# Ten loads of the transfer queue moved later in a fused attention and feed-forward kernel

## The chip, the cores and the metric

The kernel runs on one core of one Trainium2 chip. The metric is the device time of one execution in microseconds (us); the median of several runs is compared. A profile of one execution shows where the time goes.

## The reference

The kernel computes an attention of two parts and feeds its output, token by token, into a feed-forward layer. Per batch (8) and head (8), with 576 positions and a head size of 64:

```python
q_d = q.reshape(B, H, Sd, 4, D).mean(axis=3)        # the same for k and v: pooled by four
out_d = sm_attn(q_d, k_d, v_d)                      # softmax attention of 144 x 144
out_up = np.repeat(out_d, 4, axis=2)
mask = np.abs(pos[:, None] - pos[None, :]) < 4      # a band of 7 positions
out_local = np.matmul(softmax(where(mask, scale * q @ k.T, -1e9)), v)
x = (out_up + out_local)                            # then to tokens x 512
h = x @ w_in                                        # 4608 x 512 times 512 x 2048
g = h - np.tanh(h)
out = g @ w_out                                     # 2048 x 512
```

Inputs and output are 32-bit floats; the kernel multiplies in bf16.

## The kernel before, in words

The work is cut into 32 pairs of heads, four pairs to a batch (pair p belongs to batch p // 4), and eight blocks of the feed-forward layer, one per batch. For one pair the steps are:

- loads from HBM, issued by SyncE (SP): k and q into a buffer `st` (`load_qk`, L389, 256 KB each), v as two halves, one per head, into `vst` (`load_v`, L415, 160 KB each; for pairs 5 to 8 into borrowed space that the profile names gT and S), from pair 12 on a second copy of v for pooling, `v4` (`load_v4`, L425, the profile's tile v, 256 KB), and once per batch the last 64 positions of k and q (`load_rest`, L401) and of v (`load_vr`, L432, tile vr, 128 KB);
- casts to bf16 into `qr` (L551) and, once per batch, `rr` (L541); v is cast into `vw` (`prep_v`, L477);
- a transpose of k and q. For pairs 0 to 7 TensorE does it; from pair 8 on it is a DMA transpose that SP issues (`kq<-qr`, L602; the rest per batch `rT<-rr`, L596). ScalarE or VectorE then copies the rest in (L624) and k into `kt` (L629, L630), and two additions make pooled q and k (L639, L644);
- pooling of v: for pairs 0 to 11 with a matmul on TensorE (`pool_v`, L508) and a copy (L512), for later pairs with additions (L489, L493). The last positions of v are pooled per batch by three steps (`pool_vr`: L439, L443, L446);
- scores (L702, L712, L718), exponentials (L723, L727, L731), the band mask (L758), the product with v (L772), the division (L788, L790), the way back to channels by TensorE (L815) or a DMA transpose (L827), and the join into `xT` (L808).

For a block of the feed-forward layer, `mm1` (L849) multiplies `xT` with `w_in`, ScalarE takes the tanh (L861) and VectorE subtracts (L864); the second product is L1143 for block 0, later L1285 in a form with seven products in place of eight, for which sums of weights (L1194) and of tokens (L1220) are made first.

The order of all work is written out by hand. Every step is registered in a `Plan` (`P.op`) with what it reads and writes. `Plan.emit` then issues the steps in the order of the string `TURNS`, in which each step is a number of two characters. Each engine works through its own steps in that order, and so does SP: a transfer further ahead in its queue is issued first, and one that must wait holds all behind it. Steps on different engines meet only at the data that they share (and at the pairs in `BEHIND`, which keep two engines off a shared port). `ENGINES`, `BANKS` and `FILL` choose engines, PSUM banks and filler matmuls.

In the queue of SP the transposes and the loads stand mixed. From pair 8 on, SP issues a transpose only after the casts into `qr` are done, and loads behind it wait with it. The loads that matter here are written in `TURNS` as follows: 6q and 6s are k and q of pair 10, 6u the first half of its v (6w is the second), 7P k of pair 11, 7T the first half of its v, 9x vr of batch 3, Ab v4 of pair 12, AV q of pair 13, AX the first half of its v, B2 q of pair 14.

Of the kernel before, what the change touches and what calls it, by code (L numbers as in the profile page):

```python
# [101 lines left out]
def kernel(  # L102
# [51 lines left out]
    TURNS = (  # L154
        "0I0J0G0H0E0F0K0L0Q0R0O0P0W0X0e0f000307060405010M0N0S0T0Y0Z0g0h0a0b0U0V0C1011021215130D0A"
        "16171H1P18140i1J1Q191I0k0c1j1k1A1R1f1d1T0m090l0o1K1N1L1M1l222R1B1O1n1p2I2J1u1v0B231S1C24"
        "2G2n1h1W6q0n26252T2p2K2L2S1D27281U1g1V1w0q1y2Z2U1z0y2V2W391o2a292X081q1E1F1X1e0j1G3A0d0z"
        "1r1s1x202M3N3P6u212b1m2c0p2d2g2z1Y1Z2Y2y2e31322A332B2C3B3C2r2s340s1t300r3D2t5e5k2f1a2O2v"
        "2P372u2w2D1b1c3E3F2E2F3536385Q2o2h0u5S3G3H3R5U3d2i2j3e3I3J2k3j3p3k2l2m3K3L3v3M2Q3w5I3f5P"
        "5R3q2H3r3g5E3l3m3S5T3s5F3x3h3i3y3n3o5V0t3t3u414243445H5J5f5L3Q3z404748494A5X0w4D4J4E4F4G"  # L160
        "5M5O5K5N5g3T6445464K4L4M4B3O63654H2q1i4C4N5w6668675v0v4P696B4I5m4Q4V4W4b4c4d4e4O4f0x5x5z"
        "5y4h4i4R4S3V5B5C5D4T6160624j4X4Y4Z5W5Y4g4U4k4l2N2x6e6g6U4n4t5Z4a5a3X4m4u4v4z4w4x4o50516T"
        "52533Y544p4q5s5t4y4r55566V6W6X6Y576A6C6b6c6d3Z3a5b3W5h4s58595l6D6Z5c7A6a7f887B3b3c8d6E6F"
        "72898e5A5G6Q6R966G6H5d6f6h6i7C7D6j7g979C7F9D6k6l7l7E7I7m8j6m6n6o8E8F5n717473768k6p757T6K"
        "9x7r7s6I3U5u6y6s9IAb8p7G7H6L8K9J7P7x7y6v6z7778CB5i5q6w6xCFCD5o6M7J7K7L9O9P8q8v8wCG796J7M"
        "5r8L9f9a8Q8x9Q8R6O9Z9bAV7z7N7O7X6r9g9h6t9v8S9i9m7Q7Y7b9t7R7SCC5j9T9w9U9VCE7c7h7n9k7Z7o7a"
        "7i7d7e9c9j5p6S9W7t7u806PCI7p9X9l9Y9nAd7j7k7q7v8184859d9e829u9o9pAe7wAAABAC9q9r9s838A8B9z"
        "A1AGAHAg86878C8G8H8IAIAJAK8D6N8J8M70Ah8V8N8O8ZBD8aAMAD8fAE8bAmA7A8AF8WAiAn8g8X8P8hALAoAp"
        "Aq8Y8c8i8l8m8n8o8rANAOAPAjAk8s8tAt8u8y8z9091A2BFAWDyEL7VB2AXBGATA0BEBIB09yDt7U7WBcA9BMBN"
        "IgIh92BA989E93BaB3BbArAs9FBBAlENEO94CJEMBOBPBgBh99BQ9K95AUDx9AAuAcBiDzE0BJ9G9L9BBqB1EaBH"  # L170
        "BKBrBLCHE39HA5A6CLCMEJEKAv9MBsBdAwE4B8B9BtAYBRBkBlByBTEb9NE5A3A4BjE6E7BzEcEdBSCREACSCKAQ"
        "8T8UE8C0E1C1CYARBUC6CZCoE2C7C8CpBVF8BWCuC9CAEgCvEHEIASAxD0EiIcIdAyBXEhEkD2AZAaBYDuD3BZB6"
        "B7AfF7EjAzD8EPEQElEVD9ERESEeDvBmEfIeIfBuE9BvF9FAEmDEBnEBBwFDB4B5DGEnBxDHFfEwExBoDMEXEYEC"
        "IFDNEDCXEWEuEvC2F2C3ETEUDSCaFEC4BpCbBCCgIGC5F3ChFVFWFeFFCmFGFgEEEFCNFICnCTFHCUFTFUDTFBFJ"
# [1382 lines left out]
```

## Time and profile before

| | |
|---|---|
| median of three runs | 311.76 us (310.28 to 312.50) |
| the profiled execution, its own time | 310.58 us |
| its span, first to last instruction | 308.6 us |
| TensorE busy | 295.7 us, 96% of the span |
| VectorE busy | 268.3 us, 87% |
| ScalarE busy | 223.6 us, 72% |
| GpSimd busy | 155.3 us, 50% |
| granted TensorE clock | 0.999 |
| bytes moved by DMA | 60.83 MB, 197 GB/s on average |

In the profile PE is TensorE, PEld its weight loads, DVE is VectorE, ACT ScalarE, POOL GpSimd, SP SyncE. L849 is line 849 of the kernel. `ps<-xT,w_in_sb` means that tile ps is written from xT and w_in_sb; buffer numbers are left out. A row of the timeline has the start in us from the start of the span, the duration, the instruction, the number of instructions merged into it, and in brackets the idle time of the engine before it and what ended it. SP's rows are the issue of a transfer, not the transfer itself. Sizes are in KB of 1024 bytes.

### The profile page before, as it was taken

How to read it: one execution, taken by the hardware profiler on the slowest of the kernel's cores; microseconds unless marked ns; L12 is line 12 of the kernel's file. 1: busy time of each engine (PE TensorE's matmuls, PEld its weight loads, DVE VectorE, ACT ScalarE, POOL GpSimd, SP SyncE). 2: the span in 40 equal slices, each digit the busy share in tenths (PEclk: the TensorE clock that was granted, in tenths of full speed). 3: DMA queues.
4: the chain of work that ended last, by engine and by line, in shares of the span. 5: the costliest groups of instructions: out<-in, count | busy, mean ns of one | idle time of the engine just before them, and what ended most of it. 6: DMA issues, size and time to landing. Idle time of an engine off the chain costs nothing.

```text
span 308.6 us, 8109 instructions
## 1 busy us (share of the span) xinstructions
PE 295.7 (96%) x3098; PEld 209.6 (68%) x3098; DVE 268.3 (87%) x498; ACT 223.6 (72%) x401; POOL 155.3 (50%) x210
## 2 busy tenths in 40 slices
PE   7688999988999999999999999999999999999995
PEld 2575455544587765885577755655988888889984
DVE  2689887669998988999998899899999999998784
ACT  2594985467996777988967988899866898875300
POOL 5335386018465546338874268547424264616550
PEclk9999999999999999999999999999999999999999
DMA  7999999987899899999999899999999946000333
GB/s 223 254 227 274 235 235 201 196 227 190 208 258 224 243 227 206 285 239 229 263 263 202 245 211 231 237 235 238 194 196 257 162 30 186 3 3 2 137 110 97
DMA packets 121191, 60.83 MB, mean 197 GB/s; under 512 B 88896, under 2 KB 119104, under 8 KB 121152
## 3 DMA queue, kind: packets, MB, share of 16 engines
q1 hardware_dynamic: 114656, 54.94, 76.5%
q0 software_dynamic: 4224, 4.19, 8.6%
q10 hardware_dynamic: 2272, 1.18, 1.7%
q8 instruction: 24, 0.39, 0.5%
q14 instruction: 15, 0.12, 0.1%
HBM read 44.04 MB, written 9.44 MB: 173 GB/s over the span
## 4 chain that ended last, share of the span: by engine, by line
PE 66%; DVE 7%; issue 0%; ACT 0%
PE ps L1285 27%; PE ps L849 17%; PE ps L959 8%; PE ps L772 4%; PE ps L997 4%; PE ps L702 2%; PE ps L1082 2%; DVE gT L864 2%; PE ps L1115 2%; DVE gL L1010 1%; DVE E L758 1%; PE ps L718 1%; DVE S L1220 1%; DVE gT L1220 1%; DVE ln L790 1%; PE ps L712 0%
## 5 line engine op out<-in xcount | busy, mean ns | idle before, releaser
L849 PE MATMUL ps<-xT,w_in_sb 128*128 128x512 bf16 x384 | 91.9, 379 | 0.0
L1285 PEld LDWEIGHTS <-gT 128*128 128x128 bf16 x672 | 64.5, 98 | 12.4 <-DVE gT L1220 0.2
L861 ACT ACTIVATE u<-ps 128x512 f32<-128x512 f32 x96 | 56.5, 601 | 16.9 <-PE ps L849 12.9
L864 DVE TENSOR_TENSOR gT<-ps,u 128x512 bf16<-128x512 f32 x96 | 63.2, 682 | 5.8 <-ACT u L861 4.6
L849 PEld LDWEIGHTS <-w_in_sb 128*128 128x128 bf16 x384 | 35.3, 98 | 35.4 <-issue 0.2
L551 POOL CAST qr<-st 128x512 bf16<-128x512 f32 x42 | 25.3, 614 | 39.0 <-DVE qr L551 17.0
L1285 PE MATMUL ps<-w_out_sb,gT 128*128 128x256 bf16 x336 | 43.4, 273 | 0.0
L1285 PE MATMUL ps<-Tw,gT 128*128 128x256 bf16 x336 | 42.5, 273 | 0.0
L723 ACT ACTIVATE E<-ps 128x912 bf16<-128x912 f32 x32 | 29.8, 931 | 9.0 <-PE ps L712 5.4
L790 DVE TENSOR_TENSOR ln<-ps,r 128x768 bf16<-128x768 f32 x32 | 30.5, 955 | 1.0
L629 ACT COPY kt<-kq 128x576 bf16<-128x576 bf16 x23 | 27.2, 1184 | 0.7 <-DMA kq<-qr 0.4
L758 DVE TENSOR_TENSOR E<-E,mask 128x1152 bf16<-128x1152 bf16 x30 | 23.4, 787 | 4.0 <-ACT E L727 3.7
L772 PEld LDWEIGHTS <-E 128*128 128x128 bf16 x576 | 21.5, 97 | 6.2 <-DVE E L758 1.8
L731 ACT ACTIVATE E<-ps 128x576 bf16<-128x576 f32 x32 | 21.0, 657 | 2.3 <-PE ps L718 2.3
L639 POOL TENSOR_TENSOR half<-kq 128x576 f32<-128x576 bf16 x15 | 19.2, 1279 | 6.7 <-ACT u L861 3.5
L772 PE MATMUL ps<-vw,E 128*128 128x65 bf16 x320 | 19.0, 193 | 0.7 <-DVE E L758 0.4
L477 ACT CAST vw<-vst 128x640 bf16<-128x640 f32 x23 | 16.6, 736 | 1.9 <-DMA vst<-in_v_dram 1.9
L1220 DVE TENSOR_TENSOR gT<-gT 128x2048 bf16<-128x2048 bf16 x14 | 17.3, 1232 | 0.2
L644 POOL TENSOR_TENSOR qkd<-half 128x288 bf16<-128x288 f32 x18 | 14.3, 797 | 6.0 <-PE ps L508 3.2
L1371 POOL TENSOR_TENSOR y<-y,keep 128x512 f32<-128x512 f32 x8 | 10.2, 1275 | 13.4 <-DVE E L758 4.8
L997 PE MATMUL ps<-xT,w_in_sb 128*128 128x128 bf16 x256 | 16.8, 219 | 0.0
L772 PE MATMUL ps<-vp,E 128*128 128x65 bf16 x128 | 16.2, 192 | 0.3 <-DVE vp L512 0.3
(184 smaller groups left out, 593.2 us busy)
## 6 DMA issues: line engine op xcount, KB each, us to landing
vst<-in_v_dram SPq DMA_DIRECT2D x54, 160.0 KB, 4.4
st<-in_q_dram SPq DMA_DIRECT2D x28, 256.0 KB, 3.9
st<-in_k_dram SPq DMA_DIRECT2D x28, 256.0 KB, 4.3
out_dram<-y SPq DMA_DIRECT2D x14, 512.0 KB, 4.3
v<-in_v_dram SPq DMA_DIRECT2D x20, 256.0 KB, 3.2
w_in_sb<-in_moe_w_in_dram POOLq DMA_DIRECT2D x4, 512.0 KB, 8.6
w_out_sb<-in_moe_w_out_dram POOLq DMA_DIRECT2D x4, 512.0 KB, 7.6
vr<-in_v_dram SPq DMA_DIRECT2D x8, 128.0 KB
```

The lines of the kernel that those rows point to most:

```text
L551: (eng, ns, lambda dst=dst, src=src, fn=fn: fn(out=dst, in_=src), port)
L629: ("ACT", 1180, lambda: A.copy(out=ktv, in_=src), False),
L723: A.activation(out=E[s][:, :, E0:E0 + 456], in_=at(s1)[:, :, PS0:512], func=AF.Exp, scale=SCALE)
L758: eng.tensor_tensor(out=el, in0=el, in1=mask.unsqueeze(1).to_broadcast([128, 2, S]), op=ALU.mult)
L772: T.matmul(po[:, hh, 65 * n:65 * n + 65], E[s][:, hh, e:e + 128], vv, start=start, stop=stop)
L790: op("DVE", 960, lambda: V.tensor_tensor(out=ln[s].rearrange("p n (h d) -> p h n d", d=D), in0=blocks()[:, :, :, 0:64], in1=r[s].unsqueeze ...
L849: T.matmul(at(name)[:, 0, :], w_in_sb[:, dc, fc * 128:(fc + 1) * 128], xT[dc][:, c0:c0 + S].rearrange("p (c g) -> p c g", c=4)[:, :, 0:128 ...
L861: op("ACT", 600, lambda: A.activation(out=u[us], in_=at(name)[:, 0, :], func=AF.Tanh), reads=[("hd", kb, fc)], writes=[("u", us)], uses=[n ...
L864: op("DVE", 690, lambda: V.tensor_tensor(out=gT[g][:, fc, :], in0=at(name)[:, 0, :], in1=u[us], op=ALU.subtract), reads=[("hd", kb, fc), ( ...
L959: T.matmul(at(("hz", kb, G, bk))[:, 0, 256 * x:256 * x + 256], left(k, x), right(k), start=(first and x == 0 and k == 0), stop=(k == 1), s ...
L997: T.matmul(at(name)[:, 0, 128 * f:128 * f + 128], w_in_sb[:, dc, (f0 + f) * 128:(f0 + f) * 128 + 128], xT[dc].rearrange("p (b c g) -> p b ...
L1285: T.matmul(dst, left[:, f, 128 * j:128 * j + 128], right[:, f, :], start=(first and e == 0 and f == 0 and (j == 0 or apart)), stop=(e == 1 ...
```

## The change

Ten numbers in `TURNS` stand further back; nothing else is edited, and every other step keeps its place against the rest. The rows of the string are cut anew after each move, so that the diff touches many rows; its core:

```diff
-        "2G2n1h1W6q0n26252T2p2K2L2S1D27281U1g1V1w0q1y2Z2U1z0y2V2W391o2a292X081q1E1F1X1e0j1G3A0d0z"
-        "1r1s1x202M3N3P6u212b1m2c0p2d2g2z1Y1Z2Y2y2e31322A332B2C3B3C2r2s340s1t300r3D2t5e5k2f1a2O2v"
+        "2G2n1h1W0n26252T2p2K2L2S1D27281U1g1V1w0q1y2Z2U1z0y2V2W391o2a292X081q1E1F1X1e0j1G3A0d0z1r"
+        "1s1x202M3N3P212b1m2c0p2d2g2z1Y1Z2Y2y2e31322A332B2C3B3C2r2s340s1t300r3D2t5e5k2f1a2O2v2P37"
...
-        "72898e5A5G6Q6R966G6H5d6f6h6i7C7D6j7g979C7F9D6k6l7l7E7I7m8j6m6n6o8E8F5n717473768k6p757T6K"
-        "9x7r7s6I3U5u6y6s9IAb8p7G7H6L8K9J7P7x7y6v6z7778CB5i5q6w6xCFCD5o6M7J7K7L9O9P8q8v8wCG796J7M"
-        "5r8L9f9a8Q8x9Q8R6O9Z9bAV7z7N7O7X6r9g9h6t9v8S9i9m7Q7Y7b9t7R7SCC5j9T9w9U9VCE7c7h7n9k7Z7o7a"
+        "8e5A5G6Q6R966G6H5d6f6h6i7C7D6j7g979C7F9D6k6l7l7E7I7m8j6m6n6o8E8F5n717473768k6p756K7r7s6I"
+        "3U5u6y9I8p7G7H6L8K9J7x7y6z7778CB5i5q6w6xCFCD5o6M6u6v6q6r6s6t7J7K7L9O9P8q8v8wCG796J7M5r8L"
+        "9f9a8Q8x9Q8R6O7P7Q9Z9b7z7N7O7X9g9h9v8S9i9m7Y7b9t7R7SCC5j9T9w9U9VCE7c7h7n9k7Z7o7a7i7d7e9c"
...
-        "7i7d7e9c9j5p6S9W7t7u806PCI7p9X9l9Y9nAd7j7k7q7v8184859d9e829u9o9pAe7wAAABAC9q9r9s838A8B9z"
-        "A1AGAHAg86878C8G8H8IAIAJAK8D6N8J8M70Ah8V8N8O8ZBD8aAMAD8fAE8bAmA7A8AF8WAiAn8g8X8P8hALAoAp"
-        "Aq8Y8c8i8l8m8n8o8rANAOAPAjAk8s8tAt8u8y8z9091A2BFAWDyEL7VB2AXBGATA0BEBIB09yDt7U7WBcA9BMBN"
+        "9j5p6S9W7t7u806PCI7p9X9l9Y9nAd7j7k7q7v8184859d9e829u9o9pAe7wAAABAC9q9r9s838A8B9z7T7UA1AG"
+        "AHAg86878C8G8H8IAVAWAbAcAIAJAK8D6N8J8M70Ah8V9x9y8N8O8ZBD8aAMAD8fAE8bAmA7A8AF8WAiAn8g8X8P"
+        "8hALAoApAq8Y8c8i8l8m8n8o8rANAOAPAjAk8s8tAt8u8y8z9091A2BFDyEL7VBGB2B3ATA0BEBIB0Dt7WBcAXAY"
```

(6r, 6t, 6v, 7Q, 7U, 9y, Ac, AW, AY and B3 are the landings that belong to the moved loads; they issue nothing.) The order of SP's queue that comes of it, with "tr" for a DMA transpose, "a" and "b" for the first and second half of a v, and the moved loads in capitals:

```text
before  ... q5 k5 k6 vr1 | K10 | q6 v5a v5b k7 q7 | V10a | v6a v6b rest2 k8 v7a rest2 v7b q8
        tr-rest2 tr8 | V11a | q9 | VR3 | k9 | Q10 V4-12 K11 | vr2 v8b v10b v8a v9a v9b
        tr9 | Q13 | rest3 rest3 q11 tr10 k12 q12 tr11 vr4 v11b | Q14 V13a | tr-rest3 k13 tr12 k14 q15 vr5
after   ... q5 k5 k6 vr1 q6 v5a v5b k7 q7 v6a v6b rest2 k8 v7a rest2 v7b q8
        tr-rest2 tr8 q9 k9 vr2 v8b v10b v8a v9a | V10a K10 Q10 | v9b | K11 |
        tr9 rest3 rest3 q11 tr10 k12 | V11a | q12 | Q13 V4-12 VR3 | tr11 vr4 v11b tr-rest3 | Q14 | k13 tr12 k14 q15 | V13a | vr5
```

## What was predicted

> **What bounds the kernel now.** I read the page first, then the busy time by stage, then the rows of each engine in order of time around the one stage that stands out, and last SyncE's queue in that stage. The page has the span and the share of TensorE (PE):
>
> ```profile
> span 308.6 us, 8109 instructions
> ...
> PE 295.7 (96%) x3098; PEld 209.6 (68%) x3098; DVE 268.3 (87%) x498; ACT 223.6 (72%) x401; POOL 155.3 (50%) x210
> ```
>
> An average hides where the other 4% are, so I cut the span at the places where PE stops. The columns are the stretch, its length, and the busy time of PE, of the weight loads, DVE, ACT and POOL, then the granted clock, the share of the DMA engines and what they moved in GB/s.
>
> ```profile
> 28.00:68.60 40.60, 40.55 (x352) 21.17 (x350) 30.33 (x67) 27.20 (x54) 17.02 (x24) 1.00 1.06 224
> 68.60:70.80 2.20, 0.07 (x2) 0.02 (x1) 2.20 (x4) 0.60 (x1) 2.10 (x2) 1.00 1.17 239
> 70.80:300.80 230.00, 229.69 (x2419) 170.44 (x2419) 214.14 (x361) 179.52 (x313) 124.00 (x156) 1.00 0.83 190
> ```
>
> From 28 us on PE is busy without a break, except for one hole from 68.65 to 70.78 us. Beside that hole it is idle for 0.05 + 0.31 us in 270 us. So PE sets the time, a change of transfers can win the hole and hardly more, and it loses whatever new hole it opens. The hole in the rows of PE, POOL and DVE (start, duration, instruction, in brackets the idle time before it and what ended it):
>
> ```profile
> 65.45 3.20 PE L849 MATMUL ps<-xT,w_in_sb 128*128 128x512 bf16 x14
> 70.78 0.45 PE L508 MATMUL ps<-vw,pick 128*128 128x128 bf16 x5 [2.13 <-POOL vw L477]
> ```
> ```profile
> 68.62 1.43 POOL L446 TENSOR_TENSOR vpr<-vrp,hsel 128x520 bf16<-128x520 bf16 x1 [4.14 <-DVE vrp L443]
> 70.01 0.71 POOL L477 CAST vw<-S 128x640 bf16<-128x640 f32 x1
> ```
> ```profile
> 64.73 0.69 DVE L1194 TENSOR_TENSOR Tw<-w_out_sb 128x1024 bf16<-128x1024 bf16 x1
> 67.99 0.29 DVE L439 TENSOR_TENSOR vrs<-vr 128x128 f32<-128x128 f32 x1 [2.58 <-DMA vr<-in_v_dram]
> ```
>
> Read backwards: PE's pooling of v for pair 8 (L508) waits for POOL's cast of that v (L477 out of S). That cast stands on POOL behind the spreading of vr (L446). That waits for DVE, which has finished L1194 at 65.42 and then stands idle until vr of batch 2 lands at 67.98. The transfer of vr ends this wait, 2.58 us long; S itself has landed by 70.01, when its cast starts. So I look at the queue ahead of both. SyncE's (SP) rows, each the issue of one transfer (the row at 65.86 holds two, of pair 9):
>
> ```profile
> 57.23 0.53 SPq L415 DMA_DIRECT2D vst<-in_v_dram  x1
> 57.81 0.51 SPq L389 DMA_DIRECT2D st<-in_q_dram  x1
> 58.37 0.66 SPq L432 DMA_DIRECT2D vr<-in_v_dram  x1
> 59.08 0.45 SPq L389 DMA_DIRECT2D st<-in_k_dram  x1
> 59.57 0.47 SPq L389 DMA_DIRECT2D st<-in_q_dram  x1
> 60.09 0.47 SPq L425 DMA_DIRECT2D v<-in_v_dram  x1
> 60.60 0.47 SPq L389 DMA_DIRECT2D st<-in_k_dram  x1
> 61.11 0.65 SPq L432 DMA_DIRECT2D vr<-in_v_dram  x1
> 61.80 0.45 SPq L415 DMA_DIRECT2D S<-in_v_dram  x1
> ...
> 62.86 2.95 SPq L415 DMA_DIRECT2D S<-in_v_dram  x1
> 65.86 2.21 SPq L415 DMA_DIRECT2D vst<-in_v_dram  x2
> 68.18 1.37 SPq L602 DMA_TRANSPOSE kq<-qr  x1
> ```
>
> In the order of the code these are: v of pair 11, q of 9, vr of batch 3, k of 9, q of 10, v4 of pair 12, k of 11, then vr of batch 2 (61.11), the two halves of v of pair 8 (S) with one half of pair 10 between them, two halves of pair 9, and the transpose of k and q of pair 9. Five of the seven ahead of vr are loads for later pairs, and all five are among the ten that the change moves. Their sizes, from the list of DMA issues (KB of one, median us from issue to landing):
>
> ```profile
> vst<-in_v_dram SPq DMA_DIRECT2D x54, 160.0 KB, 4.4
> st<-in_q_dram SPq DMA_DIRECT2D x28, 256.0 KB, 3.9
> ...
> v<-in_v_dram SPq DMA_DIRECT2D x20, 256.0 KB, 3.2
> ...
> vr<-in_v_dram SPq DMA_DIRECT2D x8, 128.0 KB
> ...
> kq<-qr SPq DMA_TRANSPOSE x24, 4.5
> ```
>
> **The change part by part.** No engine's instructions change, in number or order, on PE, DVE, ACT and POOL; the ten loads are the same bytes, and only SP's queue is another order.
>
> *Part 1, two loads leave the early queue* (k of pair 10 and half of v of pair 10, which stand between the loads of batch 1). What stood behind them has up to 416 KB less ahead of it. PE is idle for 0.05 us in 28.00 to 68.60, so nothing can be won there, and a load that comes earlier delays nothing: 0.
>
> *Part 2, vr and S come forward.* Ahead of vr go v of 11, vr of batch 3, q of 10, v4 of 12 and k of 11: 160 + 128 + 256 + 256 + 256 = 1056 KB, or 1.08 million bytes. The rates of this stretch, by the last figure of each row:
>
> ```profile
> 62.00:66.00 4.00, 1.00 0.98 287
> 66.00:68.00 2.00, 1.00 0.52 122
> 57.00:68.00 11.00, 1.00 0.84 226
> ```
>
> At 226 GB/s that is 4.8 us, at 287 it is 3.8 us (at 122 it would be more than there is room for). So vr lands at about 67.98 - 4.8 = 63.2, at the latest at 64.2, and S, which is ready by 70.01, at 65.2 to 66.2. DVE needs vr at 65.42: its wait of 2.58 us is gone at both ends. Then POOL's spreading starts at 68.62 - 2.58 = 66.04 and the cast at 67.43, after S has landed; it ends at 68.14, before PE comes to it at 68.65. The hole goes whole: -2.13 us, with 0.5 us of room. What is late next follows.
>
> *Part 3, the transpose of pair 9 (68.18).* Ahead of it now stand q, k of 9, vr of 2, S and both halves of pairs 9 and 10, and k and q of 10 and k of 11: twelve loads where there were thirteen, 2368 KB for 2496. It is issued about 0.57 us earlier (eight issues from 57.23 to 61.80 are 0.57 us each), at 67.6. Its consumers are ACT's L624, behind it POOL's L639:
>
> ```profile
> 72.62 0.42 ACT L624 COPY kq<-rT 128x128 bf16<-128x128 bf16 x1
> ```
> ```profile
> 73.86 1.28 POOL L639 TENSOR_TENSOR half<-kq 128x576 f32<-128x576 bf16 x1
> ...
> 83.92 0.72 POOL L477 CAST vw<-vst 128x640 bf16<-128x640 f32 x1
> ```
>
> With all engines 2.13 us earlier ACT asks for it at 70.49, and POOL comes 0.82 us behind the end of L624 (73.04 to 73.86), so 0.82 us are free. The row gives landing only an upper bound, 72.62 - 68.18 = 4.44 us; a lower one is the least landing of the v loads from 56 to 92 us:
>
> ```profile
> DMA to landing us min/median/max: 2.6/4.2/6.6
> ```
>
> So the transpose lands between 70.2 and 72.0, against 70.49 + 0.82 = 71.31: 0 to 0.7 us of stall. I take 0, since the middle, 71.1, is inside the free time.
>
> *Part 4, four loads arrive ahead of the transpose of pair 11*: v of 11, q of 13, v4 of 12, vr of 3 (800 KB). SP's rows there, and those that follow from them:
>
> ```profile
> 77.31 1.24 SPq L602 DMA_TRANSPOSE kq<-qr  x1
> ...
> 79.80 0.56 SPq L415 DMA_DIRECT2D vst<-in_v_dram  x1
> ```
> ```profile
> 83.11 0.42 ACT L624 COPY kq<-rT 128x128 bf16<-128x128 bf16 x1
> ```
> ```profile
> 85.34 0.46 PE L508 MATMUL ps<-vw,pick 128*128 128x128 bf16 x5
> ```
>
> Four issues of 0.57 us are 2.3 us; 2.13 of them are covered by the time that the engines ran ahead, so this transpose goes out near 77.3 again and the second half of v of 11 near 79.8, while ACT, POOL and PE want their data 2.13 us sooner. ACT wants the transpose at 80.98: 77.3 + 4.5 is 81.8, 0.8 us late. POOL's cast of pair 11 wants its v at 81.79 instead of 83.92; PE has 85.34 - 84.64 = 0.70 us of room behind that cast. If v lands as late as now, at most at 83.92, PE waits 2.13 - 0.70 = 1.43 us; if it lands in the 2.6 us of the quickest load, at 82.4, it waits 0. I take 0.4, nearer the low end, since between the end of that transpose (78.55) and the issue of v (79.80) SP spends 1.25 us on one load, twice the usual, and can move up.
>
> A page bears on this price. The Trainium skill, DMA: Bandwidth & Descriptors, section Specifications, gives the path into the buffer a ceiling of 435 GB/s. By that the 800 KB cost an estimated 1.9 us, less than the engines' lead, and the sum would be -2.13 instead of -1.7. The row above has 287 GB/s at its best stretch, and at that the 0.82 million bytes are 2.9 us; the row decides here.
>
> *Part 5, q of pair 14 and half of v of pair 13* go behind transposes of batch 3 and pair 12, which come one or two issues earlier for it. A transpose that comes earlier delays nobody, and both loads are for pairs well behind the one in work: 0, with the hole of a late load, as in part 4, as the bound above.
>
> Later in the span SP waits for the engines ahead of its transposes, so its queue moves up with them; the largest such entry of SP's list of waits (total us, times, longest):
>
> ```profile
> SPq L827 <- DVE r L788: 10.3, 3, 6.2
> ```
>
> PE's 0.31 us of idle time in 230 us show no transfer that it waits for there. I count nothing.
>
> Sum: -2.13 + 0.4 = -1.7 us. The profiled execution took 310.58 us (span 308.6 and 2.0 around it), so 308.9; the median of the three runs, 311.76, lies 1.2 us above it, and 311.76 - 1.7 = **310.0 us**.
>
> **Rivals.** *A, absorbed.* The 2.13 us are won and given back at pairs 9 to 11, by parts 3 and 4 at their high ends: 0.7 + 1.43 = 2.13, net 0, **311.8 us**. For it: the room at each place is 0.5 to 0.8 us, less than the lead. Against it: both must be at the ends of their bounds. *B, slower.* The six v loads now stand nearly in a row ahead of the transpose of pair 9. SP's issue of such loads stuck when they were stacked: from 62.86 to 68.18 three took 5.32 us, 1.77 each where 0.57 is usual. If all six stick so, the transpose goes out at 57.23 + 6 x 0.57 + 6 x 1.77 = 71.3 and lands up to 4.44 us later, at 75.7; it is wanted at 70.49 + 0.82, so PE stands 4.4 us and the kernel loses 2.3 net: **314.0 us**. At the longest single issue, 2.95 us each, it would be far over 1%. It decides once that transpose goes out after 69.0. Against it: there were six v loads in the block before, too, and three of them stuck. *C, the change does not do it:* S comes late although vr is early. S is 1120 KB into the block, 1.15 million bytes; only near 100 GB/s would it still land at 70, a lower rate than the slowest row's 122. Even at 122 (9.4 us, plus the 2.6 of a landing, 69.2, cast to 69.9) 0.9 us of the hole would go: **310.9 us**.
>
> **How the numbers follow.** About 1% (3.1 us) is what a measurement of this kernel can tell from no change: below 308.6 is faster, above 314.9 slower. My forecast (0.8 to 2.5 us won, 2.5 being all idle time of PE after 28 us) has 0.58, C 0.05, A 0.20, B and its like 0.17, two thirds of it above 1%. Three runs of the kernel scatter from 310.28 to 312.50, so a median may lie 1 us off either way; that gives faster by over 1% its 0.08, since no mechanism does. So 0.08 faster, 0.81 within 1%, 0.11 slower. The range goes from 309.3 (all idle time won) less 1.0 for scatter, 308.3, up to 313.2, which takes in A with its scatter and the mild half of B.
>
> **What would show it.** Right: PE's L508 near 68.7 us with no idle time before it, DVE's L439 starting right behind L1194 at 65.4, vr of batch 2 issued third in the block that begins at 57.2; a small new wait of PE before the L508 of pair 11 (near 83.2), under 1 us. Wrong: ACT's L624 near 70.5 idle for over 0.8 us on the transpose; SP issues of over 2 us each between 60 and 66; PE idle for over 1 us anywhere from 70 to 90; or idle time after 90 us, which would mean that the transfers do not move up with the engines.

## The result, and the profile after

The changed kernel takes 313.78 us (median of 7 runs, 312.71 to 314.76), the kernel before, beside it, 310.28 us (7 runs, 308.78 to 312.50). The ratio is 1.0104, with a 95% interval from 1.0062 to 1.0145. Predicted were 310.0 us and a range up to 313.2: the time went the other way, past the end of the range by 0.6 us. The profiled execution took 313.88 us, 3.30 more than that of before.

The page of the changed kernel: the span, the busy time of the engines, and the granted clock of TensorE (PE) in 40 slices.

```profile
span 311.9 us, 8113 instructions
...
PE 297.7 (95%) x3098; PEld 211.3 (68%) x3098; DVE 267.9 (86%) x498; ACT 223.6 (72%) x401; POOL 156.4 (50%) x210
...
PEclk9999999999979999999999999999999999999999
```

PE (TensorE) is busy 2.0 us longer with the same 3098 instructions, and the twelfth slice (85.8 to 93.6 us) shows the clock at 7 tenths. The span cut at the place where PE stops now (columns as before: stretch, length, busy time of PE, weight loads, DVE, ACT, POOL, clock, DMA share, GB/s):

```profile
28.00:83.00 55.00, 54.96 (x495) 29.20 (x492) 46.06 (x96) 39.56 (x79) 25.51 (x35) 1.00 1.11 212
83.00:87.10 4.10, 0.17 (x4) 0.16 (x3) 3.40 (x5) 0.72 (x2) 3.87 (x5) 0.99 1.54 221
87.10:300.00 212.90, 212.64 (x2241) 160.38 (x2241) 193.68 (x326) 166.49 (x287) 111.39 (x142) 0.99 0.83 189
```

One hole again, 15 us later than the old one. PE's rows at the old hole (L508 of pair 8), at the new one (L508 of pair 11) and right behind it:

```profile
68.58 0.45 PE L508 MATMUL ps<-vw,pick 128*128 128x128 bf16 x5
...
87.03 0.69 PE L508 MATMUL ps<-vw,pick 128*128 128x128 bf16 x5 [3.93 <-POOL vw L477]
87.52 3.32 PE L997 MATMUL ps<-xT,w_in_sb 128*128 128x128 bf16 x32
```

The L508 of pair 8 has no idle time and stands 2.20 us earlier (70.78 before): the old hole is gone. The L508 of pair 11 waits 3.93 us for POOL's cast of its v, and stands 1.69 us later than before (85.34). The 32 matmuls L997 behind it take 3.32 us, 104 ns each. Measured against the same matmuls of before PE is 3.25 us late at 90.4 us, and stays so to the end. So the account is -2.20 at pair 8, +3.89 at pair 11 (from 2.20 us early to 1.69 us late) and +1.56 for the L997 at a lower clock: +3.25.

### The profile page after: what moved, and what is told of

The parts are those of the page before. It is cut to its first block, busy times and chain, and to the rows that moved or that the text cites. A ratio compares the mean times of both kernels' runs of the same rounds, so it can differ in the third digit from the quotient of the medians.

```text
span 311.9 us, 8113 instructions
## 1 busy us (share of the span) xinstructions
PE 297.7 (95%) x3098; PEld 211.3 (68%) x3098; DVE 267.9 (86%) x498; ACT 223.6 (72%) x401; POOL 156.4 (50%) x210
## 4 chain that ended last, share of the span: by engine, by line
PE 83%; DMA 8%; DVE 3%; SPq 2%; POOL 1%; issue 1%; ACT 0%; POOLq 0%
PE ps L1285 27%; PE ps L849 23%; PE ps L959 8%; PE ps L997 5%; PE ps L772 5%; PE ps L1143 4%; PE ps L702 3%; DMA Tw<-in_q_dram 2%; PE ps L1115 2%; DMA st<-in_k_dram 2%; DMA kq<-qr 2%; PE ps L1082 2%; DMA vst<-in_v_dram 2%; PE ps L815 1%; PE ps L718 1%; SPq L389 1%
## 5 line engine op out<-in xcount | busy, mean ns | idle before, releaser
L849 PEld LDWEIGHTS <-w_in_sb 128*128 128x128 bf16 x384 | 35.3, 98 | 35.3 <-issue 0.2
L551 POOL CAST qr<-st 128x512 bf16<-128x512 f32 x42 | 25.2, 612 | 40.9 <-DVE qr L551 17.0
L629 ACT COPY kt<-kq 128x576 bf16<-128x576 bf16 x23 | 27.2, 1184 | 1.4 <-DMA kq<-qr 1.2
L758 DVE TENSOR_TENSOR E<-E,mask 128x1152 bf16<-128x1152 bf16 x30 | 23.6, 793 | 4.1 <-ACT E L727 3.7
L639 POOL TENSOR_TENSOR half<-kq 128x576 f32<-128x576 bf16 x15 | 19.2, 1278 | 9.6 <-DVE Tw L1194 3.6
L997 PE MATMUL ps<-xT,w_in_sb 128*128 128x128 bf16 x256 | 18.1, 229 | 0.0
L1220 DVE TENSOR_TENSOR gT<-gT 128x2048 bf16<-128x2048 bf16 x14 | 17.2, 1231 | 0.2
L997 PEld LDWEIGHTS <-w_in_sb 128*128 128x128 bf16 x256 | 16.7, 103 | 0.8
L1010 DVE TENSOR_TENSOR gL<-ps,u 128x512 bf16<-128x512 f32 x12 | 12.0, 1019 | 5.8 <-ACT u L1008 5.8
```

What stands on the lines that cost most here:

```text
L551: (eng, ns, lambda dst=dst, src=src, fn=fn: fn(out=dst, in_=src), port)
L629: ("ACT", 1180, lambda: A.copy(out=ktv, in_=src), False),
L758: eng.tensor_tensor(out=el, in0=el, in1=mask.unsqueeze(1).to_broadcast([128, 2, S]), op=ALU.mult)
L849: T.matmul(at(name)[:, 0, :], w_in_sb[:, dc, fc * 128:(fc + 1) * 128], xT[dc][:, c0:c0 + S].rearrange("p (c g) -> p c g", c=4)[:, :, 0:128 ...
L997: T.matmul(at(name)[:, 0, 128 * f:128 * f + 128], w_in_sb[:, dc, (f0 + f) * 128:(f0 + f) * 128 + 128], xT[dc].rearrange("p (b c g) -> p b ...
```

## The experiments

The kernel before was measured again beside every group of runs. Its medians there are 309.67 to 309.94 us, while the times in the expectations start from 310.3 us. So a run is best read by its ratio to the kernel before; the changed kernel has 1.0104.

What feeds the hole is read from POOL's rows before it.

```profile
79.62 0.61 POOL L551 CAST qr<-st 128x512 bf16<-128x512 f32 x1 [0.68 <-DVE E L758]
83.23 1.17 POOL L551 CAST qr<-st 128x512 bf16<-128x512 f32 x2 [3.00 <-DMA kq<-qr]
84.36 0.96 POOL L439 TENSOR_TENSOR vrs<-vr 128x128 f32<-128x128 f32 x1
85.27 1.71 POOL L477 CAST vw<-vst 128x640 bf16<-128x640 f32 x1
```

The cast of q of pair 13 (L551 at 83.23) overwrites the buffer `qr` that the transpose of pair 11 still reads; it waits 3.00 us for that transpose, and the sum for vr of batch 3 (L439) and the cast of v of pair 11 (L477) stand behind it. But the second half of that v (below: v11b) also landed only at 85.13 by the semaphore events, 0.14 us before its cast. So two theories fit (the transpose alone, v11b alone), and a third: both are late together.

### Which of the late transfers makes the hole

Edit, as the order of SP's queue (the transposes are "tr"; all else as in the changed kernel):

```diff
-k12 v11a q12 q13 v4-12 vr3 tr11 vr4 v11b
+k12 v11a q12 tr11 q13 v4-12 vr3 vr4 v11b
```

> The changed kernel with one thing moved: the transpose of pair 11 stands ahead of q of pair 13, v4 of pair 12 and vr of batch 3, which go right behind it; the second half of v of pair 11 (v11b) has the same bytes ahead of it as before. Three theories of the hole of 3.93 us that PE has before the L508 of pair 11. T (the transpose alone): POOL's cast into qr waits 3.00 us for it, and the cast of v of pair 11 stands behind; with the transpose landed near 79.5 instead of 83.08 the hole is under 0.5 us, the clock stays at 1.00, and the time is 310.3 - 2.2 = 308.1 us. V (v11b alone, landed at 85.13): nothing changes, hole over 3.4 us, 313.8 us. W (both, tied: 85.27 is when POOL is free and 85.13 when the data is there): POOL's L551 no longer waits for the transpose, but the cast of v still starts at about 85.1 to 85.5, hole over 3.4 us, 313 to 314 us.

Measured: 312.64 us, ratio 1.0088 (1.0058 to 1.0117). POOL, and PE:

```profile
82.38 1.17 POOL L551 CAST qr<-st 128x512 bf16<-128x512 f32 x2 [2.62 <-DMA st<-in_q_dram]
83.52 0.46 POOL L439 TENSOR_TENSOR vrs<-vr 128x128 f32<-128x128 f32 x1
83.91 1.26 POOL L477 CAST vw<-vst 128x640 bf16<-128x640 f32 x1
```
```profile
85.22 0.45 PE L508 MATMUL ps<-vw,pick 128*128 128x128 bf16 x5 [2.60 <-POOL vw L477]
```

PE's hole is 2.60 us, which neither T nor V nor W expected. The transpose landed at 78.76 and nobody waited for it, but the same cast then waited 2.62 us for its other input, q of pair 13, which now stood behind the transpose.

```diff
-k12 v11a q12 q13 v4-12 vr3 tr11 vr4 v11b
+k12 v11a q12 v11b q13 v4-12 vr3 tr11 vr4
```

> The changed kernel with one thing moved: the second half of v of pair 11 stands ahead of q of 13, v4 of 12, vr of 3 and of the transpose of pair 11, which keeps all of them, and v11b too, ahead of it. T: the transpose lands at 83 to 84, the hole stays at 3.9 to 4.8 us, 313.5 to 315 us. V: v11b lands near 80, hole under 0.5 us, 308.1 us. W: as T, POOL's cast of v starts behind the wait for the transpose at 85.3 to 86.2 although its data has been there for 5 us; 313.5 to 315 us.

Measured: 314.72 us, ratio 1.0158 (1.0135 to 1.0181). v11b landed at 78.95, and its cast began 6.5 us later:

```profile
83.41 1.17 POOL L551 CAST qr<-st 128x512 bf16<-128x512 f32 x2 [3.32 <-DMA kq<-qr]
84.55 0.96 POOL L439 TENSOR_TENSOR vrs<-vr 128x128 f32<-128x128 f32 x1
85.45 1.71 POOL L477 CAST vw<-vst 128x640 bf16<-128x640 f32 x1
```

PE's hole is 4.26 us. V falls: v11b alone does not make the hole.

```diff
-k12 v11a q12 q13 v4-12 vr3 tr11 vr4 v11b
+k12 v11a q12 tr11 v11b q13 v4-12 vr3 vr4
```

> The changed kernel with the transpose of pair 11 and then v11b ahead of q of 13, v4 of 12 and vr of 3. T and V: nothing that they name is late, hole under 0.5 us, 308.1 us. W: the hole of 3.9 us shrinks by more than half and the clock stays at 1.00; a third one may be late now: vr of batch 3, last of the five, lands at 83 to 84, its sum on POOL (L439) stands ahead of the cast of v, which then starts at 84 to 85 and leaves PE 0.9 to 1.9 us idle: 309 to 310.3 us.

Measured: 312.25 us, ratio 1.0087 (1.0056 to 1.0119). The hole is 1.56 us and the clock stays at 1.00 behind it, as W expected, but for another cause than the vr that W named:

```profile
83.14 1.17 POOL L551 CAST qr<-st 128x512 bf16<-128x512 f32 x2 [2.12 <-DMA st<-in_q_dram]
```

It is q of pair 13 again. The time is about 2 us above W's upper end: in this profile L718 waits 0.88 us on POOL, and PE another 1.32 us at 180.10 on ACT's copy of y (L1307), whose cause is open. So it is no single transfer. POOL needs q13, the transpose, vr3 and v11b in this order, and whichever stands last in the burst is late.

### Taking the loads out of the burst

```diff
-tr9 rest3 rest3 q11 tr10 k12 v11a q12 q13 v4-12 vr3 tr11 vr4 v11b
+tr9 vr3 v11a rest3 rest3 q11 tr10 k12 q12 q13 tr11 vr4 v11b v4-12
```

> The changed kernel with three of the four loads of part 4 out of the way: vr of 3 and the first half of v of 11 go right behind the transpose of pair 9 (SP waits there from 68 to 71.6 anyway), v4 of 12 right behind v11b; q of 13 stays ahead of the transpose of pair 11. T, V and W all expect the transpose to land by 81 and v11b by 83, a hole under 0.5 us, clock 1.00, 308.1 us, unless the two loads delay the transpose of pair 10 (now landed at 74.42), which would show as idle time of PE between 73 and 80. A fourth theory, D: the 2.2 us of part 2 are lost downstream whatever stands ahead of pair 11's transpose; then 310.3 us.

Measured: 308.66 us, ratio 0.9969 (0.9947 to 0.9991). POOL has no wait for a transfer:

```profile
79.90 1.72 POOL L551 CAST qr<-st 128x512 bf16<-128x512 f32 x3 [0.68 <-DVE E L758]
81.58 0.46 POOL L439 TENSOR_TENSOR vrs<-vr 128x128 f32<-128x128 f32 x1
81.98 0.72 POOL L477 CAST vw<-vst 128x640 bf16<-128x640 f32 x1
```

PE has no hole before L508 any more; its longest wait behind that is 0.42 us at 91.62. Theory D (the gain is lost downstream whatever stands there) falls, though by the ratio only 1.0 us is won and not 2.2. In this profile PE is idle for 0.75 us between 90 and 300 us, against 0.25 in the kernel with part 2 alone (below); the rest of what is missing is open. One load less gives a size:

```diff
-k12 v11a q12 q13 v4-12 vr3 tr11 vr4 v11b
+k12 v11a q12 q13 vr3 tr11 vr4 v11b v4-12
```

> The changed kernel with one of the four loads of part 4 out of the way: v4 of pair 12 (256 KB) goes right behind v11b. By bytes (256 KB at 226 GB/s are 1.2 us) the transpose of pair 11 lands at 81.9 instead of 83.08 and v11b at 84.0 instead of 85.13, POOL's chain from L551 to the cast of v moves up by 1.2 us, and the hole shrinks from 3.9 to 2.7 us; 2.6 us in the run with the transpose first still brought the half clock, so 313.8 - 1.2 = 312.6 us. If only the number of loads ahead counted (six to five), 0.6 us: 313.2 us.

Measured: 311.28 us, ratio 1.0035 (1.0008 to 1.0062).

```profile
83.00 1.17 POOL L551 CAST qr<-st 128x512 bf16<-128x512 f32 x2 [2.21 <-DMA kq<-qr]
84.13 0.46 POOL L439 TENSOR_TENSOR vrs<-vr 128x128 f32<-128x128 f32 x1
84.53 0.72 POOL L477 CAST vw<-vst 128x640 bf16<-128x640 f32 x1
```

PE's hole is 1.65 us, less than the 2.7 expected, and the clock stays at 1.00 behind it. The wait for the transpose shrank by 3.00 - 2.21 = 0.79 us, between the 1.2 expected by bytes and the 0.6 by count. The rest of the gain is not a transfer: L439 and the cast took 0.46 and 0.72 us where the changed kernel has 0.96 and 1.71, 1.49 us less. 0.79 + 1.49 = 2.28 is the whole of 3.93 - 1.65. A part is given back: PE waits 0.88 us at the next L718 for POOL.

### POOL beside DVE

In the changed kernel DVE sums the tokens at that moment:

```profile
84.19 0.82 DVE L758 TENSOR_TENSOR E<-E,mask 128x1152 bf16<-128x1152 bf16 x1
84.93 1.47 DVE L1220 TENSOR_TENSOR S<-gT 128x2048 bf16<-128x2048 bf16 x1
```

The edit makes the sum wait for the cast:

```diff
-XWX6 XcXP Z5Yy ZqZ4 ZpZH
+XWX6 XcXP Z5Yy ZqZ4 ZpZH CJA9
```

(in `BEHIND`; CJ is that L1220, A9 the cast of v of pair 11)

> The changed kernel with one wait added: VectorE's sum of tokens (L1220 into S, 1.47 us), which runs from 84.93 to 86.40 beside POOL's L439 and its cast of v of pair 11, starts only behind that cast. Theory S (POOL is slowed beside it: L439 0.96 us where it takes 0.46 alone, the cast 1.71 where it took 0.72): the cast starts at 85.15, when v11b lands, and takes 0.72, so the hole goes from 3.93 to about 2.8 us and the time to 312.7 us; if the idle share of the clock's stretch falls enough for 1.00 to stay, to 311.1. Rival (the cast of 1.71 is long for another cause, or the sums are then late for PE): 313.8 us or more.

Measured: 312.93 us, ratio 1.0101 (1.0071 to 1.0131). The median is near the first value of S, but by the ratio nothing is won against the changed kernel (1.0104), so the time decides neither for S nor for its rival. The rows decide:

```profile
84.64 0.96 POOL L439 TENSOR_TENSOR vrs<-vr 128x128 f32<-128x128 f32 x1
85.55 0.71 POOL L477 CAST vw<-vst 128x640 bf16<-128x640 f32 x1
```
```profile
86.30 2.28 DVE L1220 TENSOR_TENSOR S<-gT 128x2048 bf16<-128x2048 bf16 x1 [1.01 <-POOL vw L477]
```

Without L1220 beside it the cast takes 0.71 us, and PE's hole is 2.95 us, with the clock at 1.00 behind it. L439 still takes 0.96 beside L758. The sum itself now takes 2.28 us (L1220 takes 1.23 on average in the changed kernel) beside POOL's L639 (from 86.23), which takes its usual 1.27. Of each such pair, the one that started second was held longer. The Trainium skill, SBUF — State Buffer, section Who interferes with whom, says that a DVE instruction with two inputs in SBUF contends with a GpSimd instruction that reads SBUF. L1220 adds two parts of gT, and 1.71 against 0.71 agrees.

### The clock

The edit puts 16 matmuls on PE ahead of the late L508; the queue is untouched.

```diff
-        "15717 1S25"
+        "15717 1S25 BA616"
...
-            T.matmul(bank[:, b, :], warm[:, 0:128], warm, start=True, stop=True)
+            w = w_in_sb[:, 0, 0:512] if b == 6 else warm
+            T.matmul(bank[:, b, :], w[:, 0:128], w, start=True, stop=True)
```

> The changed kernel, its queue untouched, with 16 matmuls of 128x512 on constant weights put on PE ahead of the L508 of pair 11 (their product goes to a PSUM bank that nobody reads). They leave no data earlier, so L508 still starts near 87.0. Theory I (the half clock comes from PE's idle time): the clock stays at 1.00, the L997 behind run at 56 ns each, and 1.56 us come back: 313.8 - 1.6 = 312.2 us. Rival N (the clock falls at that place for another cause): 0.50 for 3.4 us again, 313.8 us.

Measured: 313.31 us, ratio 1.0108 (1.0067 to 1.0150).

```profile
82.61 3.62 PE L1526 MATMUL ps<-w_in_sb 128*128 128x512 bf16 x16
87.77 0.45 PE L508 MATMUL ps<-vw,pick 128*128 128x128 bf16 x5 [1.54 <-POOL vw L477]
88.05 1.95 PE L997 MATMUL ps<-xT,w_in_sb 128*128 128x128 bf16 x32
```

Theory I holds in the rows: the same 32 L997 take 1.95 us instead of 3.32, and all four executions had a granted clock of 0.999 or more. In the time the expected 1.6 us did not come back (the ratio is 1.0108, against 1.0104). In the profiled execution L508 started later still (87.77 for 87.03). The transpose landed 7.67 us after its issue instead of 6.56, so that POOL's two casts L551 now stood beside L1220:

```profile
84.02 2.62 POOL L551 CAST qr<-st 128x512 bf16<-128x512 f32 x2 [3.71 <-DMA kq<-qr]
```
```profile
84.53 1.63 DVE L1220 TENSOR_TENSOR S<-gT 128x2048 bf16<-128x2048 bf16 x1
```

They took 2.62 us instead of 1.17. PE was also idle for 0.86 us between 240 and 300 us, 0.46 of it in one wait for VectorE (L808). Why the transpose landed later under the same queue is open, and so is the price of the half clock in the time of the whole kernel: the 1.56 us are read from rows.

### One part at a time

Part 4 alone, on the kernel before:

```diff
-tr8 v11a q9 vr3 k9 q10 v4-12 k11 vr2 ... tr9 q13 rest3 ... k12 q12 tr11
+tr8 q9 k9 q10 k11 vr2 ... tr9 rest3 ... k12 v11a q12 q13 v4-12 vr3 tr11
```

> The kernel before with part 4 alone: the first half of v of 11 goes behind k of 12, and q of 13, v4 of 12 and vr of 3 go right ahead of the transpose of pair 11, as in the changed kernel; the other six loads stay. Theory W (the transpose of pair 11, v11b and what POOL has queued behind them): since v of 11, vr of 3 and v4 of 12 also leave the block ahead of vr of 2 (544 KB, 2.5 us at 226 GB/s against a wait of 2.58), the hole of pair 8 goes too, and the hole of 3 to 4 us at pair 11 with the half clock is there: 313 to 314 us. Rival M (it takes all ten, by the sum of the traffic): hole at pair 11 under 2 us, 310 to 311.5 us.

Measured: 314.32 us, ratio 1.0123 (1.0080 to 1.0165). The hole at pair 8 is gone and this one is there:

```profile
87.86 0.45 PE L508 MATMUL ps<-vw,pick 128*128 128x128 bf16 x5 [3.92 <-POOL vw L477]
```

The four loads of part 4 alone make the whole loss (1.0123, against 1.0104 for all ten). Part 2 alone:

```diff
-tr8 v11a q9 vr3 k9 q10 v4-12 k11 vr2 v8b v10b v8a v9a v9b tr9 q13
+tr8 v11a q9 vr3 k9 vr2 v8b v10b v8a v9a v9b q10 k11 v4-12 tr9 q13
```

> The kernel before with part 2 alone: q of 10, k of 11 and v4 of 12 (768 KB) go behind the v loads of pair 9, still ahead of the transpose of pair 9; all else stays, so v of 11 and vr of 3 keep their early places and ahead of the transposes of pairs 9 and 11 nothing is added. If the gain of part 2 can be kept on its own: vr of 2 lands at 64.5, the hole of pair 8 goes, none opens at pair 11, 310.3 - 2.1 = 308.2 us. Theory D (lost downstream in any case, the room at pairs 9 to 11 being 0.5 to 0.8 us): 309.5 to 310.3 us, with PE idle before the scores of pair 9 or before the L508 of pair 11.

Measured: 308.40 us, ratio 0.9948 (0.9917 to 0.9978).

```profile
28.00:68.00 40.00, 39.96 (x351) 21.25 (x351) 31.49 (x69) 26.87 (x54) 18.41 (x24) 1.00 1.11 225
68.00:90.00 22.00, 21.96 (x252) 13.77 (x249) 21.55 (x36) 19.99 (x38) 14.13 (x20) 1.00 0.94 227
```

PE has no hole at all from 28 to 90 us. By the ratio part 2 is worth 1.6 us (0.7 to 2.6), which takes in the predicted 2.13, and it can be kept. The changed kernel without part 4 should then be as good:

```diff
-tr8 q9 k9 vr2 v8b v10b v8a v9a v10a k10 q10 v9b k11 tr9 rest3 ... k12 v11a q12 q13 v4-12 vr3 tr11
+tr8 v11a q9 vr3 k9 vr2 v8b v10b v8a v9a v10a k10 q10 v9b k11 v4-12 tr9 q13 rest3 ... k12 q12 tr11
```

> The changed kernel with part 4 undone and parts 1, 2, 3 and 5 kept: the first half of v of 11 and vr of 3 are back in their early places, v4 of 12 goes behind k of 11 ahead of the transpose of pair 9, q of 13 right behind that transpose, as before. Theory W (part 4 alone made the loss): no hole at pair 8 and none at pair 11, clock 1.00, as the run with part 2 alone, 308.2 to 308.6 us. Rival P (the other moves cost something of their own, most of all the k, q and v of pair 10 that part 1 and 2 put together ahead of the transpose of pair 9): PE idle between 70 and 80 us, 309.5 us or more.

Measured: 309.48 us, ratio 0.9986 (0.9955 to 1.0016): not as good, by the medians, though its profiled execution (308.06 us, the fastest of twelve) shows no hole. Two more kernels split the difference. Parts 1 and 2 (the last kernel, with part 5 undone):

```diff
-tr11 vr4 v11b tr-rest3 q14 k13 tr12 k14 q15 v13a vr5
+tr11 vr4 v11b q14 v13a tr-rest3 k13 tr12 k14 q15 vr5
```

> The run without part 4 measured 309.48 us (ratio 0.9986), the run with part 2 alone 308.4 (0.9948), although neither profile shows a hole. They differ by part 1 (k and half of v of pair 10 to behind the v loads of pair 9) and part 5 (q of 14 and half of v of 13 further back). This kernel has parts 1 and 2. If part 1 costs the difference of 1.1 us: ratio 0.998 to 1.0, about 309.3 us, and a place in its profile where the transpose of pair 9 or the casts of pair 10 come later than PE can bear. If part 5 does, or if the difference is scatter: ratio 0.995, about 308.4 us.

Measured: 309.96 us, ratio 0.9997 (0.9973 to 1.0022). And parts 2 and 5 (the kernel with part 2 alone, with part 5 added):

```diff
-tr11 vr4 v11b q14 v13a tr-rest3 k13 tr12 k14 q15 vr5
+tr11 vr4 v11b tr-rest3 q14 k13 tr12 k14 q15 v13a vr5
```

> The kernel with part 2 alone, and part 5 besides (q of pair 14 behind the rest of batch 3, half of v of 13 five transfers further back). If part 5 costs the difference between 308.4 and 309.5 us: ratio 0.998 to 1.0, about 309.3 us, with a later landing of v of 13 or of q of 14 that some engine waits for. If part 1 does, or if the difference is scatter: ratio 0.995, about 308.4 us.

Measured: 308.21 us, ratio 0.9948 (0.9922 to 0.9973). So part 5 is free, and part 1 costs about 1.5 us here (0.9997 against 0.9948; the two intervals just touch). Its place, in the kernel with parts 1 and 2 (ACT; then the busy times from 70 to 80 us):

```profile
70.21 0.42 ACT L624 COPY kq<-rT 128x128 bf16<-128x128 bf16 x1
...
73.04 1.17 ACT L629 COPY kt<-kq 128x576 bf16<-128x576 bf16 x1 [2.41 <-DMA kq<-qr]
```
```profile
70.00:80.00 10.00, 9.26 (x85) 4.68 (x85) 8.56 (x18) 7.59 (x16) 5.19 (x8) 1.00 0.97 240
```

With k and half of v of pair 10 and v4 of 12 all ahead of it, the transpose of pair 9 is late, 2.41 us for ACT, and PE loses 0.74 us between 70 and 80, about half of the cost; where the rest lies is open. The kernel without part 4 has the same queue up to here; in its profiled execution, the fastest of twelve, ACT waited 1.29 us and PE did not stop. In the kernel with part 2 alone ACT has no wait here. In the changed kernel, where v4 of 12 is not in that burst, the wait is short:

```profile
71.53 1.19 ACT L629 COPY kt<-kq 128x576 bf16<-128x576 bf16 x1 [0.68 <-DMA kq<-qr]
```

PE does not feel it. The kernel with parts 2 and 5 beats the kernel before and the changed one; that with part 2 alone is as good.

## Why the prediction was wrong

*Part 2 was right*, in the mechanism too. Predicted -2.13, measured -2.20 us; vr of batch 2 landed at 63.01 (63.2 were predicted), DVE's L439 stood at 65.42 right behind L1194, and L508 of pair 8 had no wait.

*Part 3 came true in the changed kernel, in part by luck.* The transpose of pair 9 landed at 71.45, inside the predicted 70.2 to 72.0, and PE had no stall. But it went out at 66.25 instead of 67.6 and took 5.20 us, more than the bound of 4.44: two errors cancel. Nor is ACT's L624 its reader: it ran at 70.42, before the landing, and the wait of 0.68 us is that of L629 behind it. The upper end, 0.7 us of stall, was no bound of the mechanism: with v4 of 12 in that burst as well, ACT waited 2.41 us and PE lost 0.74 there.

*Part 4 failed: +0.4 us was taken, of 0 to 1.43, and 3.89 + 1.56 were measured.* The place was foreseen (a small new wait before the L508 of pair 11), the size was not. Its own sign of being wrong came, PE idle for over 1 us between 70 and 90 us. Four errors lie in it, in the order in which they act.

First, the landing. SP's rows in the changed kernel:

```profile
74.07 1.03 SPq L389 DMA_DIRECT2D st<-in_q_dram  x2
75.15 0.47 SPq L425 DMA_DIRECT2D v<-in_v_dram  x1
75.66 0.66 SPq L432 DMA_DIRECT2D vr<-in_v_dram  x1
76.52 1.26 SPq L602 DMA_TRANSPOSE kq<-qr  x1
...
79.00 0.38 SPq L415 DMA_DIRECT2D vst<-in_v_dram  x1
```

The transpose was issued at 76.52 and v11b at 79.00, both 0.8 us before the forecast, so the issues were not the error. But the transpose landed 6.56 us after its issue (2.82 in the kernel before, by the same semaphore events), v11b 6.13 (3.92). The prediction charged the four loads for their issues only, 2.3 us, and took landing times from stretches without a burst ahead. By the rate that part 2 used for the same kind of load, 226 GB/s, their 0.82 million bytes are 3.6 us, and the way from issue to landing grew by 3.74. What part 2 took out of one burst, part 4 put into the next, and only the first was priced by bytes. The rate fits the whole burst and not each load: without v4 of 12, whose bytes are 1.2 us, the transpose still landed 6.29 us after its issue. The Trainium skill's ceiling of 435 GB/s (DMA: Bandwidth & Descriptors, Specifications), weighed there, gives an estimated 1.9 us for the same bytes, still less. The measured delay decides against it as a price.

Second, the waiting instruction. ACT's L624 and the cast of v were named as consumers. But L624 ran at 80.91, 2.17 us before the transpose landed (83.08), so it does not wait for it:

```profile
80.91 0.42 ACT L624 COPY kq<-rT 128x128 bf16<-128x128 bf16 x1
```

The transpose also holds `qr`, and POOL's cast of q of pair 13 waits to overwrite it; the cast of v stands behind that on POOL. The prediction's upper bound ("if v lands as late as now") could not see it.

Third, POOL was pushed beside L758 and L1220: 0.96 for 0.46 and 1.71 for 0.72 us, 1.49 us. These and the 3.00 us of the wait are 4.49; the hole is 3.93, so 0.56 us were room (0.70 was predicted). They are not wholly separate: v11b landed at 85.13, so a quick L439 could have let the cast start only 0.14 us sooner. Without the work beside it the hole would have been about 2.8 us (an estimate from these rows; 2.95 with the sum behind the cast).

Fourth, the clock: 1.56 us. The sum has no term for it; the old hole of 2.13 us had left the clock at 1.00.

*Part 1 at 0* held in the changed kernel, where PE is busy for 54.96 of the 55.00 us up to the hole. But it looked only at the place that the two loads left. Where they arrive they cost about 1.5 us in the kernels with part 2 and without part 4, which keep v4 of 12 in that burst. *Part 5 at 0* is borne out. *Nothing later* is too: PE's distance to before stays at 3.25 us from 90.4 us on.

*The rivals.* A and C are out. B had the sign and nearly the time (314.0), but another place: it was to decide once the transpose of pair 9 went out after 69.0, and that went out at 66.25. And issuing is not what decides: with parts 1 and 2 it went out at 67.51 and PE still stopped, since it landed 5.45 us later.

## What to carry to other kernels

A transfer that is moved back in a queue still has to pass through it: price it twice with one rate, by the bytes that leave the first place and by the bytes that arrive ahead of the first urgent transfer behind the second. Here that gave 4.8 us for a measured 4.95 (vr of batch 2) and 3.6 for 3.74 (the transpose of pair 11), but it did not give what one load taken away would bring. For each transfer that then lands later, list not only who reads it but who waits to overwrite what it reads, and what is queued behind that instruction on its engine. A hole on TensorE may cost more than its length: in the profiled execution 3.9 us of idle time brought 1.6 us more at half clock.

## What the hardware showed

The clock goes by stretches of 3.41 us, not by the length of the hole alone. In the changed kernel its records step at 5.06, 86.98 and 90.39 us, which is 24 stretches and then one, and in every other trace the steps also lie whole stretches apart. The rows below are cut at this grid, with PE's busy time as the first number after the length and the clock third from the end. First the kernel before with its hole of 2.13 us:

```profile
69.00:72.35 3.35, 1.57 (x11) 0.87 (x11) 3.23 (x6) 1.59 (x4) 2.02 (x3) 1.00 1.04 241
72.40:75.75 3.35, 3.35 (x41) 2.03 (x40) 3.27 (x8) 2.97 (x6) 3.27 (x5) 1.00 0.59 169
```

The kernel with the transpose first, hole 2.60 us:

```profile
83.20:86.55 3.35, 1.33 (x24) 1.33 (x24) 3.04 (x4) 0.89 (x3) 3.35 (x4) 1.00 1.15 206
86.62:89.97 3.35, 3.35 (x40) 2.93 (x38) 1.02 (x1) 1.97 (x4) 3.27 (x5) 0.50 1.16 299
```

The kernel with the sum behind the cast, hole 2.95 us:

```profile
81.70:85.05 3.35, 1.67 (x14) 1.00 (x13) 3.32 (x6) 1.89 (x4) 1.54 (x3) 1.00 1.18 146
85.10:88.45 3.35, 2.13 (x37) 2.06 (x36) 2.34 (x2) 1.65 (x3) 3.27 (x4) 1.00 1.19 218
```

The longer hole, cut in two by the border of a stretch, left 1.67 and 2.13 us of busy time and cost no clock; the shorter one left 1.33 us in one stretch, and the next ran at 0.50. The changed kernel had a stretch with none and paid one stretch at 0.50. The kernel with v11b first, hole 4.26 us, paid two; the second of them followed a stretch with 2.00 us of busy time, itself at half clock. So busy time alone does not tell where the border lies. Also, early in the same execution with the sum behind the cast, a stretch with 1.75 us was followed by half clock:

```profile
20.25:23.60 3.35, 1.75 (x34) 1.29 (x31) 1.41 (x4) 2.27 (x6) 1.51 (x3) 1.00 1.09 239
23.66:27.01 3.35, 3.28 (x44) 3.01 (x44) 3.25 (x11) 1.88 (x5) 0.62 (x2) 0.50 1.18 275
```

The Trainium skill, TensorE: Matmul & The Clock Gate, section What's actually happening, has the same free-running stretch of 3413 ns and a fall after an idle one. These rows add that a stretch with 40% or even half of work can be followed by the fall.

In the changed kernel the transfers also stood almost still for 1.5 us while the transpose was outstanding, at 9 GB/s between stretches at 238 and 256. The kernel with the sum behind the cast, whose queue is the same, shows it again (5 GB/s from 81 to 82 us). No run explains why:

```profile
80.50:82.00 1.50, 1.50 (x24) 0.97 (x23) 1.50 (x4) 1.00 (x3) 0.00 (x0) 1.00 1.05 9
```
